# Transposing the block maxima from a cleared tile of 128 columns

## The chip, the cores and the metric

The kernel runs on one core of one Trainium2 chip. The metric is the device time of one execution in microseconds, lower is better; the kernel before took 725.75, 725.89 and 726.9 us in three runs, the median is 725.89.

## The reference

Two independent results stand side by side in the output. One is a spectral filter of `B_x` (2048 by 576): a two-dimensional real FFT, a product with a complex weight, and the inverse. The other is an attention with 32 heads of 18 columns over four segments of 512 positions, with a memory that is carried from segment to segment; the change touches only this one:

```python
for s in range(N):
    qs, ks, vs = q[:, :, s], k[:, :, s], v[:, :, s]
    logits = jnp.einsum("bhqd,bhkd->bhqk", qs, ks) * scale + mask
    p = _softmax(logits, axis=-1)
    a_dot = jnp.einsum("bhqk,bhkd->bhqd", p, vs)
    ...
    o = g * a_mem + (1.0 - g) * a_dot
```

The softmax needs the maximum of each row of logits, and the logits are large here, since `wq` and `wk` are scaled up by 200.

## The kernel before

The program has four stages, told by the engines' timelines. Until about 75 us the forward FFT runs on TensorE, with butterflies on VectorE (DVE). Until 283 us come the projections to Q, K and V, with the middle of the FFT as background work; Q and K go to DRAM as three bf16 parts each. Until 356 us the inverse FFT runs, with the first steps of attention between its products (the prologue). The rest is the attention loop and its tail.

Attention works on four heads at a time, called a unit `k` below (32 units: four segments, eight groups of four heads). In the loop `t` counts the 128 heads of all segments. Each turn does three things for three different heads:

- `s1(t+10)` computes logits with queries on the partitions, to find the row maxima. There are products of 512, 256, 384 and 128 streamed columns (L638), a triangular mask is added by two products of 128 columns (L647), and DVE takes maxima straight from PSUM (L642, L648) into the tiles `mg` and `mx`. The PSUM tiles come from the pool `ps1`, tag `s1`, with three buffers.
- `s2(t)` computes the logits again with keys on the partitions, now less the row maximum, in three PSUM tiles (L681; L685 and L686; L690), each of which ScalarE (ACT) turns into exponentials (L682, L687, L691). GpSimd (POOL) clears the upper triangles (L694) after the fourth head of a unit.
- `pv` multiplies the exponentials of an earlier unit with V (L709). Four heads share the array, each with weights of 32 columns and its own 32 partitions of the result.

Between them stands `mpath(k)`, once for each unit, so 32 times (L657 to L672). It brings the maxima of a unit from partitions to the free axis, because the products of `s2` subtract them through two extra rows of `Q` (rows 108 and 109, against rows of −1 in `K`). Its steps are: DVE and ACT gather 16 maxima for each partition in `mg` (4 heads by 4 blocks of queries); POOL splits them into a bf16 high part and a bf16 low part in the tile `mh`, so 32 columns (L663, L664); TensorE transposes `mh` against the bf16 identity `idb` into PSUM (L667), in a tile from the same pool and tag as those of `s1` (in the prologue from a tag of its own, `mt`); ACT copies 32 rows of the result to `mts` (L670); and a DMA from POOL's queue writes these into rows 108 and 109 of `Q` (L671). `s2` of that unit waits for this DMA at its first product (L681).

The order of work on every engine is written out by hand, by generators that are advanced step by step: in the turn of a unit's fourth head the transposition is emitted between the last product of `s1` (L638, 256 columns) and the last product of `s2` (L690, 256 columns). The transposition of a unit is emitted about one unit's length ahead of its use. Background work (loads of weights, the memory terms L763 and L778, the combination L784 to L826, the output projection L843) is spread between turns.

`begin` sets up the state of attention at the start of the prologue. The pool `sm` holds the small tiles of `s1` and `mpath`.

Of the kernel before, what the change touches and what calls it, by code (L numbers as in the profile page):

```python
# [341 lines left out]
BF=mybir.dt.bfloat16  # L342
# [42 lines left out]
class ATT:  # L385
# [270 lines left out]
    def mpath(s,k):  # L656

        nc=s.nc; n,qd=divmod(k,2); Q=s.Qs[n%3]
        mx=s.mx.pop(k); mg=s.mg.pop(k)
        nc.vector.tensor_reduce(out=mg[:,:,2:3],in_=mx[:,:,:3],axis=mybir.AxisListType.X,op=OP.max)  # L660
        nc.scalar.copy(mg[:,:,0:1],mx[:,:,3:])
        mh=s.sm.tile([128,2,16],BF,name="mh",bufs=1); mg=mg.rearrange("p h i -> p (h i)")
        nc.gpsimd.tensor_copy(mh[:,0],mg)  # L663
        nc.gpsimd.tensor_tensor(mh[:,1],mg,mh[:,0],op=OP.subtract)  # L664
        yield
        pt=s.psm.tile([128,1024],BF,name="mt",tag=s.mtag)[:32,:128]
        nc.tensor.transpose(pt,mh.rearrange("p a m -> p (a m)"),s.idb)  # L667
        yield
        mt=s.sm.tile([32,128],BF,name="mts",bufs=1)
        nc.scalar.copy(mt,pt)  # L670
        nc.gpsimd.dma_start(Q[108:110,4*qd:4*qd+4].rearrange("p h (i c) -> p (h i) c",c=128),mt)  # L671
        yield  # L672
    def s2(s,t):
# [207 lines left out]
    def begin(s,sm,sp,ps1):  # L881
        s.late=[]; s.now=-1
        s.sm,s.sp,s.ps1=sm,sp,ps1
        s.mg={};s.mx={};s.m2={};s.P={};s.vs={};s.rc={};s.am={};s.pq={};s.ux={};s.potag="post"
    def prologue(s):

        nc,io=s.nc,s.io
        yield
        s.load_v(0)
        q=s.stack_dmas(1,0)+s.stack_dmas(1,1)+s.stack_dmas(2,0)+s.stack_dmas(2,1)+[lambda: s.load_v(1)]+s.stack_dmas(3,1)  # L890
        for i in range(2): yield
        i=0
        for t in range(10):
            for _ in s.s1(t):
                for _ in range(1+(i%24==0)):
                    if q: q.pop(0)()
                i+=1
                yield
            if 2<=t<6: nc.gpsimd.dma_start(s.Ks[t-2][108:110].rearrange("p h c -> p (h c)"),io["neg1"])
            if t in (3,7): m=s.mpath(t//4); next(m)  # L900
            if t in (4,8): next(m); next(m,None)
        assert not q
# [214 lines left out]
```

## Time and profile before

| | |
|---|---|
| time, median of 3 runs | 725.89 us (725.75 to 726.9) |
| span of the profiled execution | 725.3 us |
| TensorE matmul (PE) busy | 693.1 us, 96% |
| TensorE weight load (PEld) busy | 498.8 us, 69% |
| VectorE (DVE) busy | 551.2 us, 76% |
| ScalarE (ACT) busy | 455.1 us, 63% |
| GpSimd (POOL) busy | 209.4 us, 29% |
| granted TensorE clock | 0.999 |

The span runs from the first to the last instruction of one profiled execution; the runs' times hold what lies around it too. A matmul's duration in the trace includes the time until its result is through, and consecutive matmuls overlap. How long one keeps the array is therefore read from the distance between its start and the next one's start, not from its duration. Where a row gives a shape such as 128*32, the weights have 128 rows and 32 columns.

### The profile page before, as it was taken

The numbers are of one execution on the slowest core, as the hardware profiler recorded it, in microseconds if no ns is written. First come the engines' busy times: TensorE is split into PE (matmuls) and PEld (weight loads), VectorE is DVE, ScalarE is ACT, GpSimd is POOL, SyncE is SP. The second block draws the span as 40 slices with busy tenths as digits, with TensorE's granted clock in tenths as the row PEclk, the third lists the DMA queues.
The fourth block names the chain that finished last, engine by engine and source line by source line (L and its number), as shares of the span: only waits on it lengthen the run. The fifth ranks groups of instructions, "written<-read, shape, count | busy, mean of one in ns | idle before, by whom it ended". The sixth has DMA issues, their size and how long they took to land.

```text
span 725.3 us, 14481 instructions
## 1 busy us (share of the span) xinstructions
PE 693.1 (96%) x5007; PEld 498.8 (69%) x5007; DVE 551.2 (76%) x1281; ACT 455.1 (63%) x1008; POOL 209.4 (29%) x410
## 2 busy tenths in 40 slices
PE   4998999999999999999999999999899999999897
PEld 4988779879779889999844444444565445663397
DVE  6999879899799789787587878877466875667433
ACT  3665796585586574444487777767466776567531
POOL 2111000100200112565065434444142762335310
PEclk9999999999999999999999999999999999999999
DMA  9884435545363668898537656777546675441142
GB/s 339 274 261 156 136 127 183 193 168 177 124 217 131 189 206 275 208 234 224 168 102 185 173 148 146 186 165 159 141 98 172 176 172 133 111 118 41 33 144 84
DMA packets 83245, 121.06 MB, mean 167 GB/s; under 512 B 11352, under 2 KB 50630, under 8 KB 83036
## 3 DMA queue, kind: packets, MB, share of 16 engines
q1 hardware_dynamic: 76580, 104.11, 50.5%
q0 software_dynamic: 6592, 16.03, 7.8%
q8 instruction: 39, 0.64, 0.4%
q14 instruction: 34, 0.28, 0.1%
HBM read 81.78 MB, written 38.24 MB: 165 GB/s over the span
## 4 chain that ended last, share of the span: by engine, by line
PE 76%; DVE 8%; DMA 7%; ACT 5%; issue 3%; POOL 1%; SPq 0%; ACTq 0%; DVEq 0%; POOLq 0%
PE pj L460 14%; PE pv L709 9%; PE s L638 9%; PE pjv L460 8%; PE po L843 7%; PE i L296 4%; PE i L307 4%; PE s L681 3%; PE s L685 2%; PE po L872 2%; DVE eo L125 2%; PE s L690 2%; PE pn L778 2%; PE s L647 2%; PE pm L517 2%
## 5 line engine op out<-in xcount | busy, mean ns | idle before, releaser
L642 DVE CUSTOM_DVE_ANT_0 junk<-s,x 128x512 bf16<-128x512 f32 (+1 forms) x256 | 141.2, 552 | 62.3 <-PE s L638 58.6
L694 POOL TENSOR_SCALAR_AFFINE_SELECT P<-P 128x512 f32<-128x512 f32 x128 | 78.5, 645 | 82.3 <-ACT P L682 74.6
L648 DVE TENSOR_REDUCE mx<-s 128x4 f32<-128x512 f32 x128 | 87.9, 687 | 12.8 <-PE s L647 11.0
L709 PE MATMUL pv<-P,vs 128*32 128x512 f32 (+3 forms) x1024 | 88.8, 442 | 1.0 <-POOL P L694 1.0
L682 ACT ACTIVATE P<-s 128x512 f32<-128x512 f32 x128 | 76.2, 595 | 13.7 <-PE s L681 11.0
L691 ACT ACTIVATE P<-s 128x256 f32<-128x256 f32 x128 | 49.1, 384 | 52.8 <-PE s L690 52.5
L687 ACT ACTIVATE P<-s 128x512 f32<-128x512 f32 x128 | 75.7, 591 | 0.0
L638 PE MATMUL s<-Ks,Qs 108*128 108x384 bf16 (+3 forms) x256 | 69.1, 302 | 1.1 <-DVE mx L648 0.9
L460 PE MATMUL pj<-x,wqkh 128*128 128x512 f32 x162 | 56.5, 409 | 0.0
L638 PEld LDWEIGHTS <-Qs 108*128 108x128 bf16 x320 | 31.6, 99 | 31.5 <-issue 21.9
L206 DVE TENSOR_TENSOR Z<-t,t 128x290 f32<-128x290 f32 (+1 forms) x96 | 48.4, 553 | 0.1
L206 DVE TENSOR_TENSOR t<-Z 128x580 f32<-128x580 f32 x64 | 46.1, 755 | 0.0
L507 POOL MEMSET vt<- 128x32 f32 x16 | 2.3, 161 | 150.5 <-PE pm L517 123.9
L647 PE MATMUL s<-tri,idb 128*128 128x128 bf16 x256 | 43.0, 219 | 0.0
L142 PE MATMUL f<-ftab,eh 128*128 128x290 f32 (+1 forms) x160 | 30.8, 310 | 9.4 <-DMA ftab<-ftab 9.4
L296 PE MATMUL i<-civ,Y 128*128 128x256 f32 (+1 forms) x288 | 39.2, 288 | 0.2 <-POOL Y L281 0.2
L296 PEld LDWEIGHTS i<-civ,Y 128*128 128x128 f32 (+1 forms) x288 | 36.5, 181 | 1.1 <-POOL Y L281 0.4
L709 PEld LDWEIGHTS pv<-P,vs 128*32 128x32 f32 x1024 | 22.1, 108 | 21.9 <-issue 14.5
L307 PE MATMUL i<-itab,T 128*128 128x290 f32 (+1 forms) x224 | 36.3, 305 | 0.1
L460 PE MATMUL pj<-x,wqkl 128*128 128x512 f32 x90 | 35.5, 395 | 0.0
L460 PE MATMUL pj<-xh,wqkl 128*128 128x512 f32 x90 | 35.5, 395 | 0.0
L460 PE MATMUL pj<-xh,wqkh 128*128 128x512 f32 x90 | 35.5, 395 | 0.0
(201 smaller groups left out, 1809.8 us busy)
## 6 DMA issues: line engine op xcount, KB each, us to landing
qkD<-sp SPq DMA_DIRECT2D x36, 384.0 KB
Ks<-qkD SPq DMA_DIRECT2D x72, 144.0 KB
x<-qkD SPq DMA_DIRECT2D x60, 144.0 KB
Qs<-qkD SPq DMA_DIRECT2D x60, 144.0 KB
xin<-xb SPq DMA_DIRECT2D x16, 384.0 KB
cfw<-cfw POOLq DMA_DIRECT2D x16, 384.0 KB, 4.5
civ<-civ POOLq DMA_DIRECT2D x16, 384.0 KB, 7.4
vs<-vD SPq DMA_DIRECT2D x16, 330.0 KB
```

Of the source, the lines that this page charges most:

```text
L206: v.tensor_tensor(o,a,b,op=op)
L296: nc.tensor.matmul(p[:m,k],Y[i][:,q,c*128:c*128+m],cc[:,hl,o:o+256],start=n==0,stop=n==5)
L307: nc.tensor.matmul(p,x,t,start=n==0,stop=n==6)
L460: s.nc.tensor.matmul(out,a,b,start=i==0,stop=i==len(L)-1)
L638: nc.tensor.matmul(out,Q[:108,h,128*i:128*i+128],K[:108,h,:128*(i+1)],start=True,stop=True)
L642: nc.vector.tensor_tensor_reduce(out=junk[:,:w],in0=src,in1=s.mask[:,512-w:],scale=1.0,scalar=-3.0e38, op0=OP.add,op1=OP.max,accum_out=s.m ...
L647: nc.tensor.matmul(pa[:,o+w-128:o+w],s.idb,s.tri,start=False,stop=True,skip_group_check=True)
L648: nc.vector.tensor_reduce(out=s.mx[k][:,hh],in_=pa.rearrange("p (b c) -> p b c",c=128),axis=mybir.AxisListType.X,op=OP.max)
L682: nc.scalar.activation(P[0][:,hh],p0,AF.Exp,scale=SC)
L687: nc.scalar.activation(P[1][:,hh],p1,AF.Exp,scale=SC)
L694: nc.gpsimd.affine_select(out=x,in_=x,pattern=pat+[[1,128]],compare_op=OP.is_ge,fill=0.0,base=0,channel_multiplier=-1)
L709: nc.tensor.matmul(s.pvt[32*hh:32*hh+32,128*j:],vt[:,j,19*h:19*h+32],mv[0][:,hh,mv[1]],start=j==0,stop=j==2,skip_group_check=True)
```

## The change

The tile `mh` becomes one persistent tile of 128 columns, cleared once at the start of the prologue. Only its first 32 columns are ever written after that. The transposition takes all 128 columns, so its product has 128 rows, of which ACT copies the first 32 as before.

```diff
@@ mpath
-        mh=s.sm.tile([128,2,16],BF,name="mh",bufs=1); mg=mg.rearrange("p h i -> p (h i)")
+        mh=s.mh; mg=mg.rearrange("p h i -> p (h i)")
         nc.gpsimd.tensor_copy(mh[:,0],mg)
         nc.gpsimd.tensor_tensor(mh[:,1],mg,mh[:,0],op=OP.subtract)
         yield
-        pt=s.psm.tile([128,1024],BF,name="mt",tag=s.mtag)[:32,:128]
+        pt=s.psm.tile([128,1024],BF,name="mt",tag=s.mtag)[:,:128]
         nc.tensor.transpose(pt,mh.rearrange("p a m -> p (a m)"),s.idb)
         yield
         mt=s.sm.tile([32,128],BF,name="mts",bufs=1)
-        nc.scalar.copy(mt,pt)
+        nc.scalar.copy(mt,pt[:32])
@@ begin
+        s.mh=sm.tile([128,8,16],BF,name="mh",bufs=1); s.nc.gpsimd.memset(s.mh,0.0)
```

The order of instructions on the engines stays the same, but for one more instruction on POOL.

## The prediction

> **What bounds the kernel now.** I read the page first, then the chain of waits, then the stretches, and last the timeline of TensorE around the line that is changed.
>
> ```profile
> span 725.3 us, 14481 instructions
> PE 76%; DVE 8%; DMA 7%; ACT 5%; issue 3%; POOL 1%; SPq 0%; ACTq 0%; DVEq 0%; POOLq 0%
> 356.20:664.20 308.00, 299.26 (x2468) 157.38 (x2468) 225.25 (x660) 213.21 (x509) 136.48 (x248) 1.00 0.59 147
> 415.53:423.77 8.24, 8.24 (x74) 3.97 (x73) 6.91 (x21) 6.23 (x15) 3.37 (x8) 1.00 0.68 170
> ```
>
> The chain that ended last runs 76% over PE. The third row is the attention loop without its tail, the fourth one turn of it from one transposition (L667) to the next where nothing runs in the background; the columns are length, then PE, weight loads, DVE, ACT and POOL with counts, clock, DMA share. In both PE is busy almost throughout (8.24 of 8.24 us), DVE 6.91, ACT 6.23, at the full clock of 1.00. So time taken off TensorE's own issue in attention should come off the end, except where another engine or a DMA is last.
>
> A busy share of 100% hides that PE isn't always streaming. The timeline of TensorE (start, duration, instruction, shape as rows*columns of the weights) shows it by the distance from start to start:
>
> ```profile
> 431.67 0.33 PE L685 MATMUL s<-Qs,x 110*128 110x384 bf16 x1
> 431.83 0.22 PE L686 MATMUL s<-Qs,x 110*128 110x128 bf16 x1
> 431.98 0.86 PE L709 MATMUL pv<-P,vs 128*32 128x128 f32 x16
> ...
> 433.61 0.28 PE L638 MATMUL s<-Ks,Qs 108*128 108x256 bf16 x1
> 433.82 0.23 PE L667 MATMUL mt<-idb,mh 128*32 128x128 bf16 x1
> 433.98 0.28 PE L690 MATMUL s<-Qs,x 110*128 110x256 bf16 x1
> 434.10 0.33 PE L638 MATMUL s<-Ks,Qs 108*128 108x384 bf16 x1
> 434.27 0.22 PE L647 MATMUL s<-tri,idb 128*128 128x128 bf16 x1
> 434.33 0.22 PE L638 MATMUL s<-Ks,Qs 108*128 108x128 bf16 x1
> 434.38 0.22 PE L647 MATMUL s<-tri,idb 128*128 128x128 bf16 x1
> 434.44 0.38 PE L681 MATMUL s<-Qs,x 110*128 110x512 bf16 x1
> ...
> 435.10 0.27 PE L638 MATMUL s<-Ks,Qs 108*128 108x256 bf16 x1
> 435.21 0.27 PE L690 MATMUL s<-Qs,x 110*128 110x256 bf16 x1
> ```
>
> Among products with 128 weight columns, 128 streamed columns hold the array 0.06 us (434.27 to 434.33, 434.33 to 434.38) and 256 hold it 0.11 (435.10 to 435.21). Around L667, whose weights are 32 columns wide, both distances are longer: 0.21 before it (433.61 to 433.82) though 256 columns stream, and 0.16 after it (433.82 to 433.98) though 128 stream. Going from 128-wide to 32-wide also costs at the PV product: L686 at 431.83 with 128 columns, L709 at 431.98, 0.15 where 0.06 is usual. A change of the tile's shape stops the pipeline for about 0.1 us, and L667 makes two of them.
>
> Is it the shape, or that L667 is a transposition? The projection stage has transpositions of both kinds (L494), behind the same 512-column product L485:
>
> ```profile
> 97.78 0.38 PE L485 MATMUL pj<-sp,nid 128*128 128x512 bf16 x1
> 98.08 0.46 PE L494 MATMUL ptr<-ident,ex 64*128 64x64 f32 x4
> ...
> 106.88 0.39 PE L485 MATMUL pj<-sp,nid 128*128 128x512 bf16 x1
> 107.10 0.60 PE L494 MATMUL ptr<-ident,ex 128*128 128x128 f32 x4
> 107.46 0.48 PE L460 MATMUL pj<-x,wqkh 128*128 128x512 f32 x1
> ```
>
> Into the full 128 by 128 transposition PE goes in 0.22 us, which is what 512 columns take (434.44 to the next L638 at 434.66 likewise); into the one with 64 rows in 0.30. Transposing itself costs no stop; the other tile shape does.
>
> **The change part by part.**
>
> *The transposition (L667), 32 times.* Its weights grow from 32 to 128 columns, so its tile is that of its neighbours and both stops go. L638 to L690 across it now takes 0.21 + 0.16 = 0.37 us. After, 0.11 for L638 as at 435.10, and for the transposition itself a cost that the trace doesn't show for bf16: from below 0.06 (L647, same 128 columns, same identity, bf16), from above 0.09 (L494: four full ones in 107.46 − 107.10 = 0.36 us, but of 4-byte data). I take 0.06, since the data are bf16. So 0.37 − 0.17 = 0.20 us saved each time, at worst 0.17, and 0 if the stop belongs to something else in this line.
>
> *How many count.* I went along the chain of waits: L667 stands in it 23 times, 319.58 and 655.53 being the first and the last (start, length, what), and is missing 9 times.
>
> ```profile
> 319.58 0.16 PE mt L667
> ...
> 385.17 6.32 DMA Qs<-mts
> ...
> 449.86 0.55 DVE mx L648
> ...
> 562.54 7.12 DMA Ks<-qkD
> ...
> 655.53 0.16 PE mt L667
> ...
> 663.37 1.05 DVE ol L813
> ```
>
> The missing ones lie where something else is last: two around the DMA of 385.17, which PE awaited until 391.5; three beside DVE work as at 449.86; three beside DMAs as at 562.54; and the last of all, behind the DVE work of 663.37. A gain there only lengthens a wait. Sum: 23 x 0.20 = 4.6 us; at 0.17 each 3.9; if all 32 counted 6.4.
>
> *Do the engines behind PE follow?* One turn's rows, just after the L667 of 415.53:
>
> ```profile
> 415.69 0.28 PE L690 MATMUL s<-x,Ks 110*128 110x256 bf16 x1
> 415.99 0.08 DVE L642 DVE_READ_ACCUMULATOR2_ANT mg<- 128x1 f32 x1
> 416.02 0.38 ACT L691 ACTIVATE P<-s 128x256 f32<-128x256 f32 x1 [0.73 <-PE s L690]
> 416.36 0.69 DVE L648 TENSOR_REDUCE mx<-s 128x4 f32<-128x512 f32 x1 [0.28 <-PE s L647]
> ```
>
> ACT stood idle for 0.73 us until L690, DVE for 0.28 until L647. With both products 0.20 earlier, ACT follows in full, and DVE could start its reduction at 416.16, 0.09 after it ended the read of 415.99. It just fits, but without reserve: where DVE carries background work too, a part stays behind. I take off 0.4 us for that (two turns of the 23): 4.6 − 0.4 = 4.2.
>
> *The wider weight load.*
>
> ```profile
> L667 PEld LDWEIGHTS <-mh x32: 92/92/93, 319.5 to 664.2; 128*32 128x32 bf16 x32
> L647 PEld LDWEIGHTS <-idb 128*128 128x128 bf16 x256 | 25.1, 98 | 5.3 <-issue 2.9
> L681 PEld LDWEIGHTS <-Ks 110*128 110x128 bf16 x96 | 9.4, 98 | 3.7 <-issue 1.8 <-DMA Qs<-mts 1.6
> ```
>
> 98 ns in place of 92, under the running L638 product as L647's loads are; 32 x 6 ns = 0.2 us if that cover were gone. The Trainium skill ("TensorE: Matmul & The Clock Gate", section LDWEIGHTS) speaks against the change here: it makes the load proportional to its columns, P / 1.2 ns, so 27 ns for 32 and 107 for 128. By that, uncovered, 32 x 80 ns = 2.6 us would come off the gain; the rows contradict it with 92 against 98 ns, and nothing below uses it.
>
> *A wait that moves.* In the built program 29 weight loads of L638, some 6 to 17 products behind L667, now wait for TensorE's own semaphore, since ACT's copy reads only 32 of the 128 rows written and no longer stands for all of them. Six waits of L685 products on that semaphore go. The awaited product is L667 itself. In the turn above the place is the L638 of 435.10, whose load would run under L686, 1.2 us behind L667's start at 433.82; the nearest such place is that of 434.66, its load at about 434.44 and L667 through at 434.05. So the wait is met on arrival. L681's loads already wait so, on the DMA, and at 434.38 to 434.44 L681 follows in the usual 0.06. I take 0; if such a wait kept the load from going ahead, a load of 0.10 stands open, 29 x 0.10 = 2.9 us, and see the third rival.
>
> *The clearing.* One more POOL instruction at the start of the prologue, behind the last vt memset and the last V projection.
>
> ```profile
> L507 POOL MEMSET vt<- 128x32 f32 x16 | 2.3, 161 | 150.5 <-PE pm L517 123.9 <-DMA vD<-vt 16.6 <-PE c L162 5.4
> L399 POOL MEMSET zst<- 126x160 f32 x3 | 0.6, 259 | 0.0
> 283.99 0.11 POOL L508 MEMSET vt<- 128x14 f32 x1
> 286.62 2.21 POOL L281 TENSOR_TENSOR Y<-Z,Y 128x512 fp32r<-128x512 f32 x2 [2.52 <-ACT Y L280]
> 292.76 0.46 DVE L314 TENSOR_TENSOR yout<-E,i 128x290 f32<-128x290 f32 x1 [0.52 <-PE i L307]
> ```
>
> 0.16 to 0.26 us by the two memsets, inside the 2.52 us that POOL waits for ACT; were that gap gone, it would delay the second split by 0.26. The 192 bytes that the tile grows also move waits on stores of V from the second yout (L314) to the first, at 292.76, 8.8 us after the last vt tile was begun; I take 0, and DVE stood idle there for 0.52.
>
> **The rivals.**
>
> *Half is absorbed.* DVE (6.91 of 8.24 us, and 0.09 to spare in the turn above) or the DMAs of Qs take over once PE is quicker. For it: that margin, and the 9 turns already lost. Against it: 0.28 and 0.73 of idle time behind PE. 23 x 0.10 = 2.3 us: 723.6.
>
> *All 32 count*, the stalls being short: 6.4 us, 719.5. Against it: the chain.
>
> *The change doesn't do what it says*: the stop at L667 comes with a bf16 transposition, whatever its width. For it: no full bf16 transposition stands in the trace. Against it: L494 and L709. 725.9.
>
> *Slower: the weight loads on TensorE's own semaphore.* At 29 places in attention the load would no longer run ahead, PE would empty before it (0.1, as at a change of shape) and then load in the open (0.10): 29 x 0.20 = 5.8, against 4.2 gained, 727.5. It decides from 4.2 / 29 = 0.145 us each. Against it: L681, at 0.06 behind a met wait.
>
> **How the numbers follow.** The span is 725.3 us, the median of the runs 725.9, so 0.6 lie around it; 725.9 − 4.2 = 721.7. Chances: the forecast 0.65 (720.3 to 722.8), half absorbed 0.17, all count 0.07, no effect 0.05, the slower one 0.06. The range from 719.9 to 724.2 takes in the forecast with its bounds 3.9 and 4.6, the absorbed case and most of the larger gain. A measurement of this kernel can tell about 0.2%, 1.45 us, so faster means under 724.4: 0.65 + 0.17 + 0.07 less 0.02 for the edge of the absorbed case, 0.87; no difference 0.07; slower 0.06.
>
> **What would show it.** Right: L638 to L667 to L690 in the timeline at 0.11 and 0.06 in place of 0.21 and 0.16; the quiet turn at 8.04 in place of 8.24 us; L667's weight load near 98 ns. Wrong: the 0.16 behind L667 still there (no effect); turns of 8.24 with a longer gap at L681 or L638 ended by ACT or DVE (absorbed); L638 products behind the new waits starting over 0.1 us late (slower); DMA waits longer than the one at 391.5.

## The result, and the profile after

The changed kernel takes 723.35 us (median of 13 executions, 720.52 to 725.15) against 725.98 (13 executions, 723.4 to 726.9): the medians differ by 2.63 us, and the ratio is 0.9962 with a 95% interval of 0.9947 to 0.9976, so 0.38% less. The forecast was 721.7 us, the range 719.9 to 724.2. Two of the ten executions of e4 below ran in a slower state (743.19 and 769.35 us at a clock of 0.92 and 0.85) and are left out of its numbers.

The lines that answer to those of before come from the page (span, chain by engine) and from the stretches from one transposition to the next (columns as before):

```profile
span 721.9 us, 14482 instructions
PE 75%; DVE 8%; ACT 6%; DMA 5%; issue 3%; POOL 2%; SPq 0%; ACTq 0%; DVEq 0%; POOLq 0%
408.31:416.35 8.04, 8.04 (x75) 3.94 (x73) 6.91 (x21) 6.22 (x15) 3.37 (x8) 1.00 0.72 171
388.82:400.27 11.45, 9.63 (x74) 4.49 (x73) 7.42 (x24) 6.70 (x15) 3.72 (x8) 0.85 0.81 198
```

The quiet turn is down from 8.24 to 8.04 us with the same work on DVE and ACT. But one turn, the one with the long DMA wait, is up: 11.45 us where the kernel before took 9.75, and its mean clock is 0.85 (last but two columns). The timeline of TensorE in the quiet turn shows where the 0.20 us went, and the other rows show the weight load and the clearing:

```profile
416.23 0.28 PE L638 MATMUL s<-x,Qs 108*128 108x256 bf16 x1
416.35 0.22 PE L667 MATMUL mt<-idb,mh 128*128 128x128 bf16 x1
416.41 0.27 PE L690 MATMUL s<-x,Ks 110*128 110x256 bf16 x1
...
417.46 0.22 PE L686 MATMUL s<-x,Ks 110*128 110x128 bf16 x1
417.52 0.27 PE L638 MATMUL s<-x,Qs 108*128 108x256 bf16 x1
417.63 0.27 PE L690 MATMUL s<-x,Ks 110*128 110x256 bf16 x1
```

```profile
L667 PEld LDWEIGHTS <-mh 128*128 128x128 bf16 x32 | 3.2, 99 | 1.6 <-POOL am L826 0.3 <-POOL P L694 0.3 <-issue 0.2
L884 POOL MEMSET mh<- 128x128 bf16 x1 | 0.2, 204 | 0.0
```

L638 to L667 now takes 0.12 us and L667 to L690 0.06, where it was 0.21 and 0.16. The product of L638 at 417.52, whose weight load carries one of the new waits on TensorE's own semaphore, follows L686 in the usual 0.06. The weight load takes 99 ns, the clearing 0.20 us once.

### The profile page after: what moved, and what is told of

Read it like the earlier page. It is cut to its first block, busy times and chain, and to the rows that moved or that the text cites. A ratio compares the mean times of both kernels' runs of the same rounds, so it can differ in the third digit from the quotient of the medians.

```text
span 721.9 us, 14482 instructions
## 1 busy us (share of the span) xinstructions
PE 689.0 (95%) x5007; PEld 500.2 (69%) x5007; DVE 551.2 (76%) x1281; ACT 455.2 (63%) x1008; POOL 208.9 (29%) x411
## 4 chain that ended last, share of the span: by engine, by line
PE 75%; DVE 8%; ACT 6%; DMA 5%; issue 3%; POOL 2%; SPq 0%; ACTq 0%; DVEq 0%; POOLq 0%
PE pj L460 14%; PE pv L709 9%; PE s L638 8%; PE pjv L460 8%; PE po L843 7%; PE i L296 4%; PE i L307 4%; PE s L681 3%; PE s L685 2%; PE pn L778 2%; PE po L872 2%; DVE eo L125 2%; DMA Qs<-mts 2%; PE pm L517 2%; PE s L647 2%
## 5 line engine op out<-in xcount | busy, mean ns | idle before, releaser
L682 ACT ACTIVATE P<-s 128x512 f32<-128x512 f32 x128 | 76.3, 596 | 14.7 <-PE s L681 12.0
L691 ACT ACTIVATE P<-s 128x256 f32<-128x256 f32 x128 | 49.1, 384 | 49.3 <-PE s L690 49.2
L638 PE MATMUL s<-Ks,Qs 108*128 108x384 bf16 (+3 forms) x256 | 69.0, 301 | 1.2 <-DVE mx L648 0.9
L638 PEld LDWEIGHTS <-Qs 108*128 108x128 bf16 x320 | 31.5, 99 | 32.8 <-issue 23.4
L638 PE MATMUL s<-Ks,x 108*128 108x384 bf16 (+3 forms) x128 | 35.6, 309 | 0.9 <-DVE mx L648 0.6
```

The source lines that it names most:

```text
L638: nc.tensor.matmul(out,Q[:108,h,128*i:128*i+128],K[:108,h,:128*(i+1)],start=True,stop=True)
L682: nc.scalar.activation(P[0][:,hh],p0,AF.Exp,scale=SC)
```

## The experiments

**Width alone undone (e1).**

```diff
-        pt=s.psm.tile([128,1024],BF,name="mt",tag=s.mtag)[:,:128]
-        nc.tensor.transpose(pt,mh.rearrange("p a m -> p (a m)"),s.idb)
+        pt=s.psm.tile([128,1024],BF,name="mt",tag=s.mtag)[:32,:128]
+        nc.tensor.transpose(pt,mh[:,:2].rearrange("p a m -> p (a m)"),s.idb)
```

> The cleared tile of 128 columns stays, but only its first 32 columns are transposed, so the product is 32 by 128 again. If the shape of the tile makes the two stops: L638 to L667 to L690 at 0.21 and 0.16 us as before the change, and the time of the kernel before, 725 to 727 us. If instead the persistent tile, its clearing or the moved waits brought the gain: 0.12 and 0.06, and 723 to 724 us.

Measured: 725.62 us against 725.94 for the kernel before, ratio 1.000 (0.9985 to 1.0016). The timeline of TensorE:

```profile
415.54 0.28 PE L638 MATMUL s<-x,Qs 108*128 108x256 bf16 x1
415.75 0.23 PE L667 MATMUL mt<-idb,mh 128*32 128x128 bf16 x1
415.91 0.28 PE L690 MATMUL s<-x,Ks 110*128 110x256 bf16 x1
```

0.21 and 0.16 again. The cleared tile, its memset and its place in SBUF are worth nothing that shows (the interval is about 1.1 us wide to either side); the gain is the width's. With the width the moved waits go back as well, so e1 doesn't test those alone.

**A tile of 64 columns (e12), and narrow transpositions in pairs (e11), wide ones in pairs (e8).** In e12 the cleared tile has 64 columns and 64 of them are transposed; in the pairs the same line is issued twice, in the kernel before and in the changed one.

```diff
-        s.mh=sm.tile([128,8,16],BF,name="mh",bufs=1)
+        s.mh=sm.tile([128,4,16],BF,name="mh",bufs=1)
...
-        pt=s.psm.tile([128,1024],BF,name="mt",tag=s.mtag)[:,:128]
+        pt=s.psm.tile([128,1024],BF,name="mt",tag=s.mtag)[:64,:128]
@@ e11, e8
         nc.tensor.transpose(pt,mh.rearrange("p a m -> p (a m)"),s.idb)
+        nc.tensor.transpose(pt,mh.rearrange("p a m -> p (a m)"),s.idb)
```

> The changed kernel with a cleared tile of 64 columns, so a tile of 128 by 64. Theory (any change of shape stops the pipeline): L638 to L667 at 0.21 and L667 to L690 at 0.16 us, as with 32 columns. Rival (only the narrow quarter does): 0.12 and 0.06.

> The kernel before, with every 32-column transposition issued twice in a row into the same result. Theory (a stop at each change of the tile's shape, none between equal shapes): L667 to the second one at 0.06 us, then 0.16 to L690. Rival (each narrow transposition has stops of its own): 0.16 to 0.21 between the two.

> The changed kernel with every transposition issued twice in a row into the same result. Theory: the second one, 128 by 128 among tiles of the same shape, adds 0.06 us, no stop; L667 to L667 at 0.06. Rival (a bf16 transposition costs more than a product of its size): 0.09 or more.

The timelines of TensorE, first of e12, then of e11 (L668 and L691 are the second transposition and the old L690), then of e8:

```profile
415.80 0.28 PE L638 MATMUL s<-x,Qs 108*128 108x256 bf16 x1
416.01 0.24 PE L667 MATMUL mt<-idb,mh 128*64 128x128 bf16 x1
416.19 0.28 PE L690 MATMUL s<-x,Ks 110*128 110x256 bf16 x1
```

```profile
433.62 0.28 PE L638 MATMUL s<-Ks,Qs 108*128 108x256 bf16 x1
433.84 0.23 PE L667 MATMUL mt<-idb,mh 128*32 128x128 bf16 x1
433.90 0.22 PE L668 MATMUL mt<-idb,mh 128*32 128x128 bf16 x1
434.06 0.28 PE L691 MATMUL s<-Qs,x 110*128 110x256 bf16 x1
```

```profile
433.22 0.22 PE L667 MATMUL mt<-idb,mh 128*128 128x128 bf16 x1
433.28 0.22 PE L668 MATMUL mt<-idb,mh 128*128 128x128 bf16 x1
433.33 0.28 PE L691 MATMUL s<-Qs,x 110*128 110x256 bf16 x1
```

With 64 columns both stops are there, 0.21 and 0.18. Two narrow ones in a row stand 0.06 apart, and the stops come once before and once after the pair. A wide one costs 0.06. So each change of the tile's shape costs about 0.1 us, and the instruction itself is as cheap narrow as wide. The three had one execution each, so their times decide nothing (726.25, 725.76 and 722.95 us).

**The changed kernel again (e2).**

> The changed kernel as it is, on the same chip as the next two. Theory: 720 to 722 us in executions whose mean clock is 0.999 or more, 723 to 725 in those where a half-clock window of 3.4 us follows the wait for the Qs rows near 391 us. Rival (the gain is absorbed all through attention): the times don't part by the clock.

722.96 us against 725.94, ratio 0.9959 (0.9941 to 0.9977). The theory came true in part. Of its eight executions the three below a clock of 0.998 took 724.1 to 724.5 us, as expected, but of the five above it only two lie between 720 and 722; the profiled one took 723.03 us at a clock of 1.000. With the 13 executions of the result it makes 21: the 13 with a mean clock of 0.998 or more have a median of 722.0 us, the 8 below 724.0, and the groups overlap (720.5 to 724.5, 723.35 to 725.15). The kernel before parts in the same way: over the three comparisons that list its clocks 48 executions at 0.998 or more have a median of 725.6, 12 below it 727.3. At the same clock the change is thus worth 3.6 and 3.3 us. That the lower clock comes more often after the change (8 of 21, against 12 of 60) is too few executions to be shown.

**Issuing L671 from SyncE's queue (e3, e4).**

```diff
-        nc.gpsimd.dma_start(Q[108:110,4*qd:4*qd+4].rearrange("p h (i c) -> p (h i) c",c=128),mt)
+        nc.sync.dma_start(Q[108:110,4*qd:4*qd+4].rearrange("p h (i c) -> p (h i) c",c=128),mt)
```

> The kernel before, with the DMA of mts to Qs (L671) issued from SyncE's queue in place of GpSimd's, so that it no longer stands behind the four selections and the wol splits. Theory: the wait of 1.7 us near 391 goes or shrinks below 0.5, the turn there takes 8.3 in place of 9.75, about 724.4 us; no half-clock window before the tail. Rival (DMAs are what bounds there, whoever issues): the wait stays over 1.2 us, 726.

> The changed kernel with the same move of L671 to SyncE's queue. Theory (32 times 0.20 us, hidden in the result by the wait near 391 and the half-clock window behind it): 718 to 719.5 us, some 5 to 6 us under the kernel before with the same move. Rival (half is absorbed along the whole of attention): 2.5 to 3 us under it, 721.5.

732.14 (six executions) and 727.8 us (eight), both slower than the kernel before (725.94). The wait near 391 did go: the turn there took 8.25 us in e3, as expected. But the next turn took 12.93. The small DMA now stands in the queue with the loads of Q and K, and between 380 and 410 us of e3 that queue waits 4.3 us for ACT ahead of it. The list of waits of e3, then of e4 (engine and line, what it waited for, us in total, times, longest):

```profile
PE s L638 <- DMA Qs<-qkD: 3.0, 1, 3.0
```

```profile
PE s L638 <- DMA Qs<-qkD: 2.3, 1, 2.3
```

The expected cure made a longer wait one turn on. The two versions differ by the change alone: 4.3 us, with intervals that don't overlap (1.0048 to 1.0110 and 1.0003 to 1.0037 of the kernel before); in the profiles 0.7 of it is the shorter wait.

**Starting the output weights later (e5, e6).**

```diff
-        bg=[s.late_setup(tp)]
+        bg=[]
...
+            if t==12: bg.append(s.late_setup(tp))
```

> The kernel before, with the background setup of the output weights (loads of wo on SyncE's queue, splits on ACT and POOL) begun at turn 12 of the loop instead of turn 0. In the kernel before the third of these loads holds SyncE's queue from 360 to 373 us with the DMA engines 15% busy, and the loads of Q, K and pq crowd behind it until 425. Theory: without that the waits for DMAs between 380 and 425 go, 723 to 725 us. Rival (the crowd comes from the loads themselves): waits stay, 726.

> The changed kernel with the same later start. Theory (0.20 us in nearly every turn, of which waits for DMAs before 425 us take the first nine): 718 to 720 us, 4.5 to 6 under the kernel before with the same later start, no half-clock window before the tail. Rival (a fixed half is absorbed in any case): 2.5 to 3 us under it.

735.14 (four executions) and 731.37 us (seven): both much slower. The turn of 389 did get shorter in e5 (8.81 us where the kernel before took 9.75), but new waits stand at 409 and 426, so the later start moved the waits and lengthened them. (In the kernel before the DMA engines are 35% busy from 360 to 373 us, and 14% only from 364 to 373.) The list of waits of e5 names them:

```profile
PE s L638 <- DMA Ks<-qkD: 6.2, 1, 6.2
PE s L681 <- DMA x<-mts: 2.6, 1, 2.6
```

Between the two medians stand 3.8 us, but with so few executions the intervals overlap (1.0062 to 1.0140 and 1.0052 to 1.0113 of the kernel before).

**Delaying the one DMA that PE waits for (e7).**

```diff
+        if k==4: nc.gpsimd.memset(s.sm.tile([128,600],F32,name="dl",bufs=1),0.0)
         nc.gpsimd.dma_start(Q[108:110,4*qd:4*qd+4].rearrange("p h (i c) -> p (h i) c",c=128),mt)
```

> The kernel before, with one clearing of 128 by 600 float32 elements on POOL (0.6 us, worked out from the two memsets) ahead of the one DMA of unit 4, on which PE waits until 391.5 us. Theory (a wait of about 2 us is followed by 3.4 us of half clock): the wait grows to 2.2 us, a half-clock window stands behind it in most executions, mean clock 0.996 to 0.997, 727.5 to 728.5 us. Rival (the window has nothing to do with the wait): 726.5, clock as before.

726.23 us, ratio 0.9994 (0.9976 to 1.0012), and 7 of 10 executions at a clock of 0.998 or more. It didn't decide anything: the clearing took its 0.61 us, but the profiled wait came out shorter (1.06 us in place of 1.43). The DMA was issued at 386.63 in place of 385.17 and landed at 392.1 in place of 391.5, so its landing isn't set by its issue alone, and PE came later too. Whether a longer wait brings the lower clock had to be read from the other traces.

**Moving the loads of pq (e9, e10).**

```diff
-            if 16<=t<21: s.pq_load(1,t-16)
+            if 24<=t<29: s.pq_load(1,t-24)
```

> The kernel before, with the five loads of pq (252 KB each) for the second segment issued in turns 24 to 28 instead of 16 to 20, so that they leave the stretch from 388 to 400 us, where the DMA engines are 82% busy and PE waits for the Qs rows. Theory: the waits between 380 and 405 go, 724 to 725 us. Rival (the loads only crowd a later stretch): 726.

> The changed kernel with the same later loads. Theory (the first nine turns keep their 0.20 us, and no half-clock window follows a wait near 391): 719.5 to 721 us, 4.5 to 5 under the kernel before with the same later loads. Rival (half is absorbed whatever the DMAs do): 2.5 to 3 us under it.

726.49 and 726.36 us: here the change is worth nothing that shows (the ratios to the kernel before are 1.0009, 0.9994 to 1.0023, and 1.0001, 0.9976 to 1.0026). PE still waited 1.22 us for the Qs rows in e9, so moving the loads of pq away doesn't remove that wait. The timeline of the profiled execution of e10 shows where its lead went:

```profile
449.32 0.28 PE L638 MATMUL s<-Ks,x 108*128 108x256 bf16 x1
450.38 2.21 SPq L622 DMA_DIRECT2D x<-qkD  x3
450.39 0.37 DVE L734 TENSOR_SCALAR ry<-ry 128x128 f32<-128x128 f32 x1 [2.43 <-DMA ry<-dD]
...
451.66 0.63 DVE L648 TENSOR_REDUCE mx<-s 128x4 f32<-128x512 f32 x1
452.21 0.68 DVE L642 CUSTOM_DVE_ANT_0 junk<-s,x 128x512 bf16<-128x512 f32 x1
452.34 0.27 PE L667 MATMUL mt<-idb,mh 128*128 128x128 bf16 x1 [2.74 <-DVE mx L648]
```

and so do its stretches (clock in the last but two columns):

```profile
448.00:452.00 4.00, 1.60 (x21) 0.69 (x20) 1.58 (x3) 1.11 (x3) 1.81 (x3) 0.92 0.63 133
452.00:456.00 4.00, 3.54 (x17) 2.09 (x17) 3.71 (x11) 2.98 (x9) 2.36 (x5) 0.50 0.64 134
456.00:460.00 4.00, 4.00 (x23) 1.32 (x21) 2.38 (x9) 2.47 (x7) 1.34 (x4) 0.72 0.60 164
```

DVE stood for 2.43 us at the head of its queue for a DMA whose use is placed a fixed number of steps after its issue (L734). It came for it at 447.96, where DVE in e9 used it at 449.53 without a wait. The reduction behind it came late, and PE waited 2.74 us for it. Meanwhile the clock fell, at 451.4: (0.08 + 0.50 + 0.28) x 4 = 3.4 us of clock lost. In e9, the same program with the narrow transposition, no DMA wait of DVE stands there in the profile, and all ten executions have a clock of 0.998 or more, against two of ten in e10. No version tried is faster than the changed kernel.

## Why the prediction was right, and where it was off

The median of 723.35 us lies in the range, but not between 720.3 and 722.8, where the forecast had a chance of 0.65: it is 1.65 above the forecast and 0.25 below the 723.6 of the rival "half is absorbed". The account of the gain was right; what takes part of it away was under-priced, and the range held because it had been made wide enough for that rival.

*The stop belongs to the shape, not to transposing: right.* e1, e8, e11 and e12 show it for bf16, of which the trace of before had no full transposition. "No effect" is out.

*0.20 us each: right.* 0.37 less (0.12 + 0.06) is 0.19, and the quiet turn lost 0.20. The price taken for the full transposition, 0.06, is measured.

*The own semaphore and the wider load cost nothing: right*, by the rows of 417.52 and 99 ns. Compared product by product, no L638 that stands 6 to 17 products behind L667 follows its predecessor more than 0.04 us later than before, apart from the turn at half clock. The slower rival is out.

*How many count: right in sum, not turn by turn.* The starts of L667 in the two profiles, from the same transposition to the same one:

| stretch (start before) | before, us | after, us | difference |
|---|---|---|---|
| 319.51 to 389.31 | 69.80 | 69.37 | −0.43 |
| 389.31 to 399.06 | 9.75 | 11.45 | +1.70 |
| 399.06 to 459.60 | 60.54 | 59.43 | −1.11 |
| 459.60 to 468.09 | 8.49 | 9.12 | +0.63 |
| 468.09 to 499.51 | 31.42 | 31.34 | −0.08 |
| 499.51 to 514.41 | 14.90 | 12.76 | −2.14 |
| 514.41 to 664.18 | 149.77 | 147.57 | −2.20 |

Together they give −3.63 us. Of the 31 turns between the 32 transpositions 16 are 0.18 to 0.22 us shorter, seven 0.08 to 0.16, four not at all, and in four PE waits for a DMA in one of the two profiles. The 27 without such a wait give 4.0 us, against 4.2 in the sum. But they aren't the turns that the chain named: of its 23 only 13 gained in full, and of the nine that it left out three did (563.45, 574.08 and 595.11). That the sum came out is luck, in that these errors cancel.

Both stops are gone in the turns that gained nothing too; there a later product starts about 0.2 us later. In two of the four it is L681, which takes the PSUM tile that ACT's L682 frees. The rows of before, then of after:

```profile
491.45 0.59 ACT L682 ACTIVATE P<-s 128x512 f32<-128x512 f32 x1
492.09 0.38 PE L681 MATMUL s<-Qs,Ks 110*128 110x512 bf16 x1
```

```profile
492.18 0.59 ACT L682 ACTIVATE P<-s 128x512 f32<-128x512 f32 x1
492.83 0.38 PE L681 MATMUL s<-Qs,Ks 110*128 110x512 bf16 x1
```

L681 starts 0.05 and 0.06 us behind the end of L682. ACT comes to L682 without a pause from L780, 1.38 us in both profiles, and L780 waits for a product ahead of the transposition (L778). So "ACT follows in full", read from the quiet turn, doesn't hold there. In the third of the four L820 waits for DVE (L785), in the fourth L843 for ACT (L845). The term for the small reserve behind PE, 0.4 us and DVE's alone, stands against a loss of 1.4 (27 x 0.20 less 4.0), of which at least 0.6 is ACT's.

*What a lengthened wait costs: this term was mis-sized.* "A gain there only lengthens a wait" priced it at nothing. The row 389.31 shows +1.70. In both profiles PE stops there for the DMA of mts to Qs; the first two rows are of before, the fence behind them of after, and the last of after's stretches:

```profile
389.88 0.22 PE L647 MATMUL s<-tri,idb 128*128 128x128 bf16 x1
391.53 0.39 PE L681 MATMUL s<-Qs,Ks 110*128 110x512 bf16 x1 [1.43 <-DMA Qs<-mts]
```

```profile
389.27 0.22 PE L647 MATMUL s<-tri,idb 128*128 128x128 bf16 x1
391.31 0.56 PE L681 MATMUL s<-Qs,Ks 110*128 110x512 bf16 x1 [1.82 <-DMA Qs<-mts]
391.67 0.63 PE L638 MATMUL s<-Ks,x 108*128 108x512 bf16 x1
392.10 0.52 PE L685 MATMUL s<-Qs,Ks 110*128 110x384 bf16 x1
```

```profile
388.00:392.00 4.00, 2.18 (x25) 1.07 (x26) 2.07 (x9) 1.79 (x7) 3.06 (x6) 0.92 1.00 232
392.00:396.00 4.00, 4.00 (x22) 1.68 (x21) 2.52 (x7) 2.63 (x6) 0.50 (x1) 0.65 0.73 189
```

PE came 0.6 us earlier, the DMA landed only 0.2 earlier, so the wait grew from 1.43 to 1.82. Behind it 512 columns take 0.43 us (391.67 to 392.10) in place of 0.22: the clock fell to half, for (0.08 + 0.35) x 4 x 2 = 3.4 us, and cost 1.7. With 0.39 of longer wait, less the 0.20 saved, that is the +1.70. One such window is about what parts 722.0 from 724.0 us above; that the executions without a profile have one is inferred from their mean clock. The +0.63 is a wait of 0.81 us for the DMA of rr at L820, new in this profile, and the −2.14 is chance: the profiled execution of before waited 1.87 us for pq at 510, the one of after didn't, nor did the one of e1, which has the narrow transposition too.

```profile
468.49 0.38 PE L820 MATMUL pb<-rr,sel 96*126 96x512 bf16 x1 [0.81 <-DMA rr<-rrD]
```

```profile
509.97 1.02 PE L763 MATMUL pd<-pq,zst 72*32 72x512 f32 x2 [1.87 <-DMA pq<-pqD]
```

*What lies around the span* was put at 0.6 us. The profiled execution of after took 723.62 us with a span of 721.9, so it is 1.7, and the profile of before was one of the longer executions, about 727.0. The forecast was made from the median and didn't suffer, but its chain of waits, with pq in it, was not that of a typical execution.

*The half clock isn't needed for the loss.* The profiles of e1 and e2, on one chip, both stay at the full clock until the tail. There the 26 turns without a wait for a DMA give 3.9 us, and the five with one (those of 381, 389, 399, 415 and 460) take back 1.9, so 2.0 are left from the first L667 to the last. PE's two largest waits for DMAs in e2:

```profile
PE s L638 <- DMA Ks<-qkD: 1.6, 1, 1.6
PE s L681 <- DMA Qs<-mts: 1.1, 2, 0.6
```

*Open:* which part of the missing 1.65 us (723.35 less 721.7) is the half-clock window and which is longer DMA waits as such, over all executions. Between e1 and e2 the change is worth 2.7 us, and 4.3, 3.8 and 0.1 in the pairs e3/e4, e5/e6 and e9/e10, whose waits are others. Removing the wait near 391 was tried in three ways; it stayed, or another came, so no pair shows the full gain in the time without such waits.

## What to carry to other kernels

In this kernel a product whose weights fill fewer columns than its neighbours' costs two stops of about 0.1 us beside its own time; padding it with cleared columns to the neighbours' shape removes them, and grouping narrow products pays the stops once. When an engine that bounds gets quicker and DMAs are issued a fixed number of turns ahead, the time between issue and use shrinks too: look which DMA lands with little to spare, and count the clock that a longer wait may cost. A profile is one execution of a kernel whose DMA waits vary by 2 us; compare turns, not spans. And the chain of waits says what was last, not by how little: an engine that ends 0.05 us ahead of PE's product doesn't stand in it, and takes the gain all the same.

## What the hardware showed that was not expected

The clock falls to half after a stop of TensorE far shorter than the window that follows. In the attention loop stops of 2.3 us and more always brought one (2.31 and 2.97 us in e4 and e3; with windows of twice the length 2.74 in e10, 6.22 and 2.58 in e5, 5.55 in e6), stops of 1.82, 1.87 and 2.00 us once out of three times.

What parts these three is where they lie, not their length. In every profile the half clock starts a whole number of steps of 3.413 us behind the first moment at full clock; in the profile of after that is 15.93 us, and the clock falls 110 steps later, at 391.39. The step that ends there and the next one (length, then PE's busy time; the clock is the last but two), and behind them two steps of e6 with a stop of 1.73 us:

```profile
387.98:391.39 3.41, 1.59 (x24) 0.91 (x25) 2.09 (x9) 1.20 (x5) 2.97 (x5) 1.00 1.03 221
391.39:394.80 3.41, 3.41 (x14) 1.63 (x14) 1.94 (x6) 2.59 (x6) 0.61 (x1) 0.50 0.79 217
```

```profile
422.78:426.20 3.42, 1.79 (x13) 1.07 (x14) 1.63 (x4) 1.76 (x5) 1.66 (x3) 1.00 0.62 172
426.20:429.61 3.41, 3.41 (x30) 1.19 (x28) 2.93 (x10) 2.73 (x7) 0.41 (x2) 1.00 0.59 165
```

After a step with PE busy for 1.59 us the clock fell (1.62 in e10), after one with 1.79 it didn't. The stop of 2.00 us, in e8, lies across two steps, with 2.04 and 2.78 busy, and nothing followed; that of 1.87 in before lies across two as well. So in the loop the clock fell where PE stood idle for 53% of a step or more, and not at 48% or less. It is not the whole rule: in the tail it fell after steps with only 25% (after) and 24% (e8) idle.

The Trainium skill ("TensorE: Matmul & The Clock Gate", section What's actually happening) has the lower clock come after at least one idle window of about 3.4 us, the window running freely. The length of 3.4 us and the free running agree with the traces here; that a whole window has to be idle doesn't, and the measurement decides.

A 64-column tile pays the same stops as a 32-column one (0.21 and 0.18 us, against 0.21 and 0.16).
